# Seven products for gate and value in two blocks, signs masked on VectorE, scores at their own scale

## The chip, the cores and the metric

One core of one Trainium2 chip runs the whole program. The time is the device time of one execution in microseconds (us). The kernel before took 1258.47 us (median of three runs, 1258.27 to 1259.04).

In the profile, PE is TensorE's matmuls, PEld its weight loads, DVE is VectorE, ACT ScalarE, POOL GpSimd and SP SyncE, whose queue issues the DMAs.

## The reference

Attention over 4 batches, 12 heads, 448 tokens and head size 64 (q and k normalised by their root mean square), then two feed-forward stages on the 1792 x 768 result. The inputs are of twice the width of float32 (each number comes as two 32-bit words).

```
q_n, k_n = rmsnorm(q, g_q), rmsnorm(k, g_k)
attn = softmax(q_n @ k_n.T / sqrt(64));  o = attn @ v
x  = o.transpose(0, 2, 1, 3).reshape(1792, 768)
x  = silu(x @ w_in) @ w_out                          # 768 -> 2048 -> 768
y  = (silu(x @ w_gate) * (x @ w_val)) @ w_out2       # 768 -> 1536 -> 768
```

## The kernel before

Nearly every product is done as three float16 matmuls: each operand is split into a high and a low half (hi x hi, hi x lo, lo x hi), summed in PSUM in float32. A weight tile of 128 rows is loaded (one `LDWEIGHTS`) ahead of each matmul.

**The order of the work** is written out by a planner: the class `Plan` gathers operations with the engines they may run on, a planned cost and a due time, and `emit` puts them on the five queues one by one. The table `TUNE` shifts due times (`OFF`, `FINE`) and names the engines that each operation may run on (letters A, D, P for ACT, DVE, POOL, and E for a way by matmuls). Each engine then works through its own queue strictly in that order. A change of `TUNE` therefore reorders everything.

**Stages in time.** Attention of batch 0 with float32 scores (0 to 120 us; four of its six head pairs, `N0 = 4`, feed the float32 matmuls of L701). From 120 us the first feed-forward product of batch 0 (`ffn1_h`, L1011) runs while the weights `w_out` are brought in; its second product (`ffn1_o`, L1051) starts near 229 us, and needs the scales of all 16 pieces of `w_out`. Then attention of batches 1 to 3 runs between the feed-forward products of the batch before. The second feed-forward stage starts near 708 us: four blocks of tokens, of 512, 512, 512 and 256. In each block `ffn2_gv` makes gate and value (L1206), and `ffn2_out` multiplies by `w_out2` (L1250 to L1252). The steady part runs from about 792 us to the end at 1258 us.

**Gate and value of one block** (`ffn2_gv`): for each of 12 column groups f of 128, six weight tiles of gate and six of value, each with three matmuls, 36 matmuls of 512 columns (256 in the last block). Then ACT makes silu (L1211), DVE multiplies with value from PSUM (L1213), ACT rounds to float16 (L1216), DVE makes the remainder (L1217), POOL or ACT scales it (L1218, L1219). `bring_x2` fetches the block's 768 x n inputs from DRAM (`x2d`) and splits them (L832, L842) during the output product of the block before.

**Weights** (`bring`): a 128 x 768 piece arrives by DMA with 64 bits a number. The exponent part is scaled by ACT, DVE or POOL (L873 to L875). The sign and the lowest bits follow one of two ways, named per piece by a letter in `TUNE`: with A or P, DVE shifts the low word (L885) and ACT (L887) or POOL (L888) rescales the high word; with D, DVE masks the sign (L879) and shifts a half word (L880). L890 joins the parts on DVE, and L892 sums the squares on ACT. `convert` then scales and splits the piece (L832 to L842), or makes its low half by matmuls with a diagonal (`pe_lo`, L676), for which `diag` writes the diagonal on POOL (L905).

**Softmax** (`softmax_pair`): DVE takes the negative row maximum of the scores (L715), a small operation scales it (L718 ACT, L719 DVE or L720 POOL), and the exponential reads scores, scale and bias (L723).

Of the kernel before, what the change touches and what calls it, by code (L numbers as in the profile page):

```python
# [45 lines left out]
    GK=('D', 'P', 'DP'),
# [1341 lines left out]
```

## Time and profile before

| what | value |
|---|---|
| median of three runs | 1258.47 us |
| the profiled execution | 1259.7 us, of which 1257.9 us are the span from the first to the last instruction |
| mean granted TensorE clock | 0.98 of full |
| PE busy, share of the span | 94% |
| DVE, ACT, POOL busy | 55%, 53%, 39% |
| DMA issues from SP's queue | the heaviest pieces are 768 KB weights |

Busy times are averages over stages with different limits, so they are to be read by stretch. A matmul's record lasts longer than the step from one matmul to the next, since matmuls are pipelined; the pace is read from runs of matmuls without a gap in the chain of work that ended last.

### The profile page before, as it was taken

Reading aid. Unit: us, or ns where it says so; the run is one execution under the profiler, and the core shown is the slowest. Engines: PE = TensorE matmul, PEld = TensorE weight load, DVE = VectorE, ACT = ScalarE, POOL = GpSimd, SP = SyncE. Lnnn points to the kernel's source line nnn. Section 1 sums busy time; section 2 is a strip of 40 time slices with the busy share of each in tenths; the row PEclk is TensorE's granted clock in tenths of the full one; section 3 lists DMA queues with packets and bytes.
Section 4 is the critical chain, followed back from the end, with each engine's and each line's share of the span. In section 5 each row is a group of like instructions: output and inputs, shape, how many; then the busy total and the mean of one; then the engine's idle time right before and its main releaser. Section 6 shows DMA issues by size and latency. Waiting matters only on the chain.

```text
span 1257.9 us, 17505 instructions
## 1 busy us (share of the span) xinstructions
PE 1178.2 (94%) x6612; PEld 599.2 (48%) x6612; DVE 687.2 (55%) x1181; ACT 669.4 (53%) x1219; POOL 492.0 (39%) x474
## 2 busy tenths in 40 slices
PE   5989987799679999999999999999999999999998
PEld 3334443344334444444445454445544555446685
DVE  4788876688756575565459887873111301112121
ACT  4989967677669865898536435652111301112131
POOL 5565456454658897677721624120000100000000
PEclk9999999799889999999999999999999999999999
DMA  7565634479877688567774455502000101000101
GB/s 193 167 155 144 220 131 145 103 174 199 184 149 144 125 191 176 110 126 149 145 238 138 146 173 180 187 1 63 26 14 1 34 26 26 1 1 22 39 1 26
DMA packets 218581, 140.61 MB, mean 112 GB/s; under 512 B 156032, under 2 KB 210816, under 8 KB 218496
## 3 DMA queue, kind: packets, MB, share of 16 engines
q1 hardware_dynamic: 218496, 139.49, 44.3%
q8 instruction: 52, 0.85, 0.3%
q14 instruction: 33, 0.27, 0.1%
HBM read 85.79 MB, written 11.01 MB: 77 GB/s over the span
## 4 chain that ended last, share of the span: by engine, by line
PE 46%; DVE 5%; DMA 2%; POOL 1%; ACT 1%; issue 1%; POOLq 0%; ACTq 0%
PE ps L1206 25%; PE ps L1051 6%; PE ps L1250 4%; PE ps L1252 4%; PE ps L1251 4%; DMA ATT<-in_moe_w_val_dram 1%; DVE W L842 1%; PE ps L816 1%; PE ps L1011 1%; PE ps L706 1%; DVE ATT L890 1%; DVE G L1030 1%; DVE ATT L880 1%; DVE ATT L879 1%; DMA ATT<-ATT 1%
## 5 line engine op out<-in xcount | busy, mean ns | idle before, releaser
L1206 PE MATMUL ps<-XT,W 128*128 128x512 f16 (+1 forms) x1440 | 294.0, 352 | 3.8 <-ACT ER L1211 1.9
L1051 PE MATMUL ps<-G,W 128*128 128x448 f16 x1152 | 240.7, 355 | 4.0 <-DVE G L1041 4.0
L1011 PE MATMUL ps<-XT,W 128*128 128x448 f16 x1152 | 234.9, 353 | 8.2 <-ACT FT L1017 1.7
L1206 PEld LDWEIGHTS <-W 128*128 128x128 f16 x1440 | 141.0, 98 | 131.0 <-issue 5.1
L1011 PEld LDWEIGHTS <-W 128*128 128x128 f16 x1152 | 110.7, 99 | 120.5 <-issue 26.0
L1051 PEld LDWEIGHTS <-W 128*128 128x128 f16 x1152 | 107.9, 98 | 122.3 <-issue 28.9
L1216 ACT ACTIVATE G<-ER 128x512 f16<-128x512 f32 (+1 forms) x48 | 27.6, 575 | 167.3 <-DVE ER L1213 162.2
L1213 DVE SCALAR_TENSOR_TENSOR ER<-ER,ST,ps 128x512 f32<-128x512 f32 (+1 forms) x48 | 32.6, 680 | 151.5 <-PE ps L1206 151.4
L723 ACT ACTIVATE ER<-ps,ST 128x448 f32<-128x448 f32 x144 | 103.1, 719 | 12.1 <-POOL ATT L745 8.8
L1218 POOL TENSOR_SCALAR G<-ER 128x512 f16<-128x512 f32 x20 | 12.6, 629 | 245.5 <-DVE ER L1217 241.2
L715 DVE TENSOR_REDUCE ST<-ps 128x2 f32<-128x896 f32 x96 | 92.4, 966 | 27.8 <-PE ps L706 23.4
L1250 PE MATMUL ps<-W,G 128*128 128x384 f16 x308 | 100.4, 326 | 0.0
L1251 PE MATMUL ps<-W,G 128*128 128x384 f16 x308 | 100.4, 326 | 0.0
L1252 PE MATMUL ps<-W,G 128*128 128x384 f16 x308 | 100.4, 326 | 0.0
L1257 DVE SCALAR_TENSOR_TENSOR ATT<-ps,ST,ATT 128x384 f32<-128x384 f32 x28 | 17.3, 618 | 151.0 <-ACT ATT L1255 151.0
L1255 ACT ACTIVATE ATT<-ps,ST 128x384 f32<-128x384 f32 x28 | 16.2, 580 | 136.7 <-PE ps L1252 136.7
L745 POOL TENSOR_TENSOR ATT<-ER,ATT 128x448 f16<-128x448 f32 x77 | 86.0, 1117 | 6.4
L706 PE MATMUL ps<-ATT 128*64 128x448 f16 x560 | 75.3, 371 | 9.1 <-ACT ER L723 4.0
L1030 DVE SCALAR_TENSOR_TENSOR G<-FT,ST,G 128x448 f16<-128x448 f32 x64 | 57.5, 907 | 20.1 <-ACT G L1022 18.2
L744 POOL TENSOR_SCALAR ER<-ER,ST 128x448 f32<-128x448 f32 x77 | 56.7, 736 | 22.8 <-ACT ATT L739 11.8
L1206 PE MATMUL ps<-XT,ATT 128*128 128x512 f16 (+1 forms) x288 | 60.4, 352 | 0.0
L739 ACT ACTIVATE ATT<-ER,ST 128x448 f16<-128x448 f32 x71 | 45.5, 660 | 20.0 <-DVE ST L731 11.7
(221 smaller groups left out, 1889.4 us busy)
## 6 DMA issues: line engine op xcount, KB each, us to landing
ATT<-in_moe_w_out_dram SPq DMA_DIRECT2D x24, 768.0 KB, 4.3
W<-in_moe_w_in_dram SPq DMA_DIRECT2D x16, 768.0 KB, 6.1
ATT<-in_moe_w_gate_dram SPq DMA_DIRECT2D x12, 768.0 KB, 4.7
ATT<-in_moe_w_val_dram SPq DMA_DIRECT2D x12, 768.0 KB, 5.9
ATT<-in_q_dram SPq DMA_DIRECT2D x24, 224.0 KB, 3.1
ATT<-in_k_dram SPq DMA_DIRECT2D x24, 224.0 KB, 3.6
ATT<-in_v_dram SPq DMA_DIRECT2D x8, 672.0 KB, 7.2
x2d<-FT SPq DMA_DIRECT2D x24, 224.0 KB, 3.5
```

What stands on the lines that cost most here:

```text
L706: nc.tensor.matmul(out=sp[64 * h:64 * h + 64, u, 0:S], lhsT=T[:, 0, t, 64 * h:64 * h + 64], rhs=T[:, a, :, 64 * h:64 * h + 64], start=(a = ...
L715: op(DVE, 1.04 * S * nt + 65, lambda sp=sp, nm=nm, nt=nt: nc.vector.tensor_reduce(nm, sp[:, 0:nt, 0:S], AX.X, ALU.max, negate=True), r=sk, ...
L723: op(ACT, 705, lambda e=e, u=u, t=t, sp=sp: nc.scalar.activation(e, sp[:, u, 0:S], AF.Exp, bias=st["nb"][:, t:t + 1], scale=eS, accum_out= ...
L744: nc.gpsimd.tensor_scalar(e, e, r1, 1.0, ALU.mult, ALU.mult)
L745: nc.gpsimd.tensor_tensor(lo, e, hi, ALU.subtract)
L1011: nc.tensor.matmul(out=ps[:, 0:S], lhsT=w[:, a, kk], rhs=xt1((b * HP + kk) % NX, x), start=(kk == 0 and s == 0), stop=(kk == KD - 1 and s ...
L1030: DVE: (t_stt(S), lambda gt=gt, hi=hi, lo=lo, s1=s1: nc.vector.scalar_tensor_tensor(lo, gt, s1, hi, ALU.mult, ALU.subtract), True),
L1051: nc.tensor.matmul(out=ps[:, 0:S], lhsT=w[:, a, P * m:P * m + P], rhs=GV1[:, f, x], start=(f == 0 and s == 0), stop=(f == NF1 - 1 and s == 2))
L1206: nc.tensor.matmul(out=ps[:, 0:n], lhsT=w[:, aa, kk], rhs=xt2(kk, x)[:, 0:n], start=(kk == 0 and s == 0), stop=(kk == KD - 1 and s == 2))
L1250: nc.tensor.matmul(out=ps[:, 0, 0:384], lhsT=hi, rhs=wh, start=(f == 0), stop=(f == NF2 - 1))
L1251: nc.tensor.matmul(out=ps[:, 1, 0:384], lhsT=hi, rhs=wlo, start=(f == 0), stop=False)
L1252: nc.tensor.matmul(out=ps[:, 1, 0:384], lhsT=lo, rhs=wh, start=False, stop=(f == NF2 - 1))
```

## The change

**Seven products.** The blocks keep their sizes, but blocks 1 and 2 (counted from 0) compute gate and value by a scheme with seven half-size products in place of eight. The input of a block is a 2 x 2 arrangement (two halves of 256 tokens, two halves of the 768 inputs); so is the weight of one f (two halves of the inputs, gate and value). Seven products of sums of such quarters give the four quarters of the result. Each product has three weight tiles and three matmuls for each, of 256 columns: 63 matmuls an f.

- `make_sums` (new) makes, for each f, four sums of weight quarters in float32 on DVE (ten additions of 384 columns, L1288 of the changed kernel), rounds them on ACT, makes the remainder on DVE (1536 columns, L1297) and stores hi and lo to a DRAM buffer `s2d` (768 KB an f).
- `bring_sums` (new) takes the place of `bring_x2` for the two blocks: three steps, each with two DMAs of 256 KB, four sums of input quarters (256 columns, L1264) and a split of 1792 columns.
- `ffn2_seven` (new) takes the place of `ffn2_gv` there: it loads the sums of each f back from `s2d` into one of two buffers, issues the products (L1329), and joins them in five DVE additions that read PSUM (L1346: three of 256 columns, two of 512). All eight PSUM banks take part.
- The output tiles `OT` shrink from four buffers to two, and `DG` and `FT` become parts of one tile `FD`, whose space the joins use later.

**Signs.** The table `WOS` names D for all 16 pieces of `w_out` (before: one piece by D alone). `diag` may run on DVE as well.

**Scores.** For the first four head pairs the scale stays in the scores: the maximum is the bias itself, and the small scaling operation is left out.

**The tables.** `TUNE` is new in nearly all entries, so that work shifts between ACT, DVE and POOL elsewhere too.

```diff
-    WOS=('P', 'P', 'P', 'AP', 'P', 'A', 'AP', 'AP', 'P', 'P', 'P', 'AP', 'AP', 'AP', 'P', 'D'),
+    WOS=('D',) * 16,
...
-    small(mult(gc, gc, g_s), ["gs"], ["gc"], 0)
+    small(lambda: nc.vector.tensor_scalar(gc, gc, 2.0 ** -25, None, ALU.mult), [], ["gc"], 0)
...
-            op(DVE, 1.04 * S * nt + 65, lambda sp=sp, nm=nm, nt=nt: nc.vector.tensor_reduce(nm, sp[:, 0:nt, 0:S], AX.X, ALU.max, negate=True),
-               r=sk, w=[("nm", i, g)], due=due)
+            own = n < N0
+            top = nb if own else nm
+            op(DVE, 1.04 * S * nt + 65, lambda sp=sp, top=top, nt=nt: nc.vector.tensor_reduce(top, sp[:, 0:nt, 0:S], AX.X, ALU.max, negate=True),
+               r=sk, w=[("nb" if own else "nm", i, g)], due=due)
+            if not own:
...
-        op(POOL, 351, lambda: nc.gpsimd.tensor_scalar(dg, ID, s1, 2.0 ** 14, ALU.mult, ALU.mult), r=["id"] + sk, w=[("dgw", c)], due=due)
+        add({POOL: (351, lambda: nc.gpsimd.tensor_scalar(dg, ID, s1, 2.0 ** 14, ALU.mult, ALU.mult)),
+             DVE: (200, lambda: nc.vector.tensor_scalar(dg, ID, s1, 2.0 ** 14, ALU.mult, ALU.mult), True)}, r=["id"] + sk, w=[("dgw", c)], due=due)
...
+    def make_sums():
...
+            for dst, terms in ((0, ((vh[:, lo], vh[:, hi], ALU.add), (vl[:, lo], ALU.add), (vl[:, hi], ALU.add))),
+                               (2, ((gh[:, lo], vh[:, lo], ALU.subtract), (gl[:, lo], ALU.add), (vl[:, lo], ALU.subtract))),
+                               (1, ((us[:, 0], gh[:, lo], ALU.subtract), (gl[:, lo], ALU.subtract))),
+                               (3, ((gh[:, hi], us[:, 1], ALU.subtract), (gl[:, hi], ALU.add)))):
...
+            op(SP, t_dma(P * 6144), lambda f=f: nc.sync.dma_start(out=s2d[P * f:P * f + P], in_=SH), r=["SHh", "SHl"], w=[("s2d", f)], due=due, late=DMA_LATE)
...
+    RING = [(PS_F[i], ("F", i)) for i in range(3)] + [(PS_X, "psx")] + [(PS_S[i][:, u], ("S", i, u)) for i in range(2) for u in range(2)]
...
+    def ffn2_seven(i, z):
...
+            op(SP, t_dma(P * 6144), lambda sb=sb, f=f: nc.sync.dma_start(out=sb, in_=s2d[P * f:P * f + P]), r=[("s2d", f)], w=sbk, due=t0 + step * (f - 2), late=DMA_LATE)
...
+                for kk in range(KH):
+                    def mm(kk=kk):
+                        for s, (aa, xx) in enumerate(((0, 0), (0, 1), (1, 0))):
+                            c = 1792 * xx + h * x
+                            nc.tensor.matmul(out=ps[:, h * o:h * o + h], lhsT=w[:, aa, kk], rhs=XW[kk][:, c:c + h],
...
+            b1, b6, b2, b57, b34 = take(), take(), take(), take(), take()
+            product(b1, 0, g[:, :, 0:KH], gk, 0)
...
+            product(b6, 0, sw[:, 1], sbk, 2)
+            plus(3, 1, b6, 0, 0, zk[0:1])
+            product(b2, 0, g[:, :, KH:KD], gk, 5)
+            plus(0, 1, b2, 0, 0, zk[0:1])
+            product(b57, 0, sw[:, 0], sbk, 1)
+            product(b57, 1, sw[:, 2], sbk, 3)
+            plus(1, 2, b57, 0, None, zk[3:4])
+            plus(3, 1, b57, 0, 2, zk[2:3])
+            product(b34, 0, sw[:, 3], sbk, 6)
+            product(b34, 1, v1[:, :, KH:KD], vk, 4)
+            plus(1, 2, b34, 0, 1, [])
...
-        ffn2_gv(i, zone(i))
+        (ffn2_seven if i in SEVEN else ffn2_gv)(i, zone(i))
+        if i == 0:
+            plan.tag = "sums"
+            make_sums()
```

**What moves in the queues.** In the listings below a row is an instruction in the order of its queue: line, operation, tile written <- tiles read, size of the output; lines are those of the kernel named, and those of the changed kernel are higher (its L882, L887, L888, L898, L914 do what L874, L879, L880, L890 and, on POOL, L905 do before).

DVE while pieces of `w_out` are converted, of before (L1030 is the low half of `ffn1_h`, L450 to L457 are scales):

```order
L885 TENSOR_SCALAR ATT<-ATT 128x768
L890 SCALAR_TENSOR_TENSOR W<-W,ATT 128x768
L1030 SCALAR_TENSOR_TENSOR G<-FT,ST,G 128x448
L450 TENSOR_SCALAR ST<-ST 128x1 x2
L890 SCALAR_TENSOR_TENSOR W<-W,ATT 128x768
L456 TENSOR_SCALAR ST<-ST 128x1 x2
```

The same place in the changed kernel:

```order
L882 TENSOR_SCALAR W<-ATT 128x768 x2
L887 TENSOR_SCALAR ATT<-ATT 128x768
L914 TENSOR_SCALAR FD<-ID,ST 128x128
L888 TENSOR_SCALAR ATT<-ATT 128x768
L887 TENSOR_SCALAR ATT<-ATT 128x768
L898 SCALAR_TENSOR_TENSOR W<-W,ATT 128x768
```

Sign, half word and join of a piece stand on DVE alone now, and the diagonals stand between them. Counted up to the first matmul of `ffn1_o`, L879 and L880 go from 2 to 17 each, L885 from 30 to 15, L887 on ACT from 16 to 10, L888 on POOL from 14 to 5, and the diagonals on POOL from 15 to 3, with 12 on DVE.

DVE from the output product of block 0 into gate and value of block 1, of before:

```order
L1217 TENSOR_TENSOR ER<-ER,G 128x512
L1257 SCALAR_TENSOR_TENSOR ATT<-ps,ST,ATT 128x384 x6
L1213 SCALAR_TENSOR_TENSOR ER<-ER,ST,ps 128x512
L1217 TENSOR_TENSOR ER<-ER,G 128x512
L1257 SCALAR_TENSOR_TENSOR ATT<-ps,ST,ATT 128x384 x2
```

In the changed kernel, early in block 1 (L1288 and L1297 are the sums of weights of a later f, L1346 the joins, L1364 and L1368 what L1213 and L1217 were):

```order
L1346 TENSOR_TENSOR G<-ps,G 128x512
L1288 TENSOR_TENSOR ATT<-ATT 128x384 x2
L1346 TENSOR_TENSOR FD<-ps,FD 128x256
L1364 SCALAR_TENSOR_TENSOR G<-G,ST 128x512
L1346 TENSOR_TENSOR FD<-ps,FD 128x256
L1346 TENSOR_TENSOR FD<-ps,FD 128x512
L1368 TENSOR_TENSOR G<-G 128x512
L1346 TENSOR_TENSOR FD<-ps,FD 128x256
L1288 TENSOR_TENSOR ATT<-ATT 128x384
L1346 TENSOR_TENSOR FD<-ps,FD 128x512
```

Two instructions an f become seven, and the sums of weights stand between them. By the count in the queues, three of the twelve f have their sums made before the output product of block 0 begins, and the other nine stand in DVE's queue during that product and block 1.

SP's queue at the same place of the changed kernel (L1299 stores sums, L1315 loads them back, L1258 loads inputs, L1412 writes the result):

```order
L1412 DMA out_dram<-ATT 64x768 x2
L1299 DMA s2d<-ATT 128x3072
L1315 DMA ATT<-s2d 128x3072
L1412 DMA out_dram<-ATT 64x768 x2
L1315 DMA ATT<-s2d 128x3072
L1299 DMA s2d<-ATT 128x3072
L1315 DMA ATT<-s2d 128x3072 x2
L1299 DMA s2d<-ATT 128x3072
L1315 DMA ATT<-s2d 128x3072 x3
```

The twelve stores and 24 loads are new, and a load can stand behind a store that waits for a sum.

## Rows read from the trace of the kernel before

**Rows 1.** The page: busy us, share of the span and instructions of each engine.
```profile
PE 1178.2 (94%) x6612; PEld 599.2 (48%) x6612; DVE 687.2 (55%) x1181; ACT 669.4 (53%) x1219; POOL 492.0 (39%) x474
```

**Rows 2.** Busy time by stretch: start:end, length, busy us and instructions, PEclk, DMA.
```profile
120.00:229.00 109.00, 91.53 (x420) 45.22 (x419) 81.38 (x163) 86.98 (x141) 56.19 (x46) 0.94 0.45 149
...
640.00:800.00 160.00, 152.94 (x794) 77.93 (x793) 137.79 (x231) 82.14 (x138) 59.56 (x42) 1.00 0.54 175
800.00:852.00 52.00, 52.00 (x245) 23.72 (x243) 39.46 (x61) 29.95 (x47) 10.00 (x10) 1.00 0.18 61
852.00:992.00 140.00, 140.00 (x721) 70.47 (x720) 27.11 (x38) 25.66 (x40) 8.05 (x13) 1.00 0.08 23
992.00:1132.00 140.00, 140.00 (x721) 70.44 (x720) 27.74 (x40) 26.02 (x41) 7.53 (x12) 1.00 0.07 19
```

**Rows 3.** The chain that ended last: start us, length us, what.
```profile
912.34 80.29 PE ps L1206 x372
...
1187.30 40.61 PE ps L1206 x372
```

**Rows 4.** Groups by form at L1206: count, busy us and mean ns, idle before.
```profile
L1206 PE MATMUL ps<-XT,W 128*128 128x512 f16 x1080 | 249.8, 379 | 3.8 <-ACT ER L1211 1.9 <-ACT FT L1055 1.8
...
L1206 PEld LDWEIGHTS <-W 128*128 128x128 f16 x1440 | 141.0, 98 | 131.0 <-issue 5.1
...
L1206 PE MATMUL ps<-XT,W 128*128 128x256 f16 x360 | 44.2, 273 | 0.0
```

**Rows 5.** Waits of PE from 792 us to the end.
```profile
PE ps L1206 <- ACT ER L1211: 1.9, 1, 1.9
```

**Rows 6.** Groups by form on DVE in gate, value and output.
```profile
L1217 DVE TENSOR_TENSOR ER<-ER,G 128x512 f32<-128x512 f32 x36 | 27.7, 770 | 17.9 <-ACT G L1216 17.8
...
L1213 DVE SCALAR_TENSOR_TENSOR ER<-ER,ST,ps 128x512 f32<-128x512 f32 x36 | 26.9, 746 | 122.3 <-PE ps L1206 122.1
...
L1257 DVE SCALAR_TENSOR_TENSOR ATT<-ps,ST,ATT 128x384 f32<-128x384 f32 x28 | 17.3, 618 | 151.0 <-ACT ATT L1255 151.0
...
L1213 DVE SCALAR_TENSOR_TENSOR ER<-ER,ST,ps 128x256 f32<-128x256 f32 x12 | 5.8, 480 | 29.2 <-PE ps L1206 29.2
...
L1217 DVE TENSOR_TENSOR ER<-ER,G 128x256 f32<-128x256 f32 x12 | 5.1, 425 | 5.8 <-ACT G L1216 5.8
```

**Rows 7.** DVE in order of time: start us, length us, instruction.
```profile
229.64 1.00 DVE L842 SCALAR_TENSOR_TENSOR W<-ATT,ST,W 128x768 f16<-128x768 f32 x1
230.57 1.08 DVE L715 TENSOR_REDUCE ST<-ps 128x2 f32<-128x896 f32 x1
```

**Rows 8.** The page: DMA issues, KB each, median us to landing.
```profile
ATT<-in_moe_w_out_dram SPq DMA_DIRECT2D x24, 768.0 KB, 4.3
...
ATT<-in_moe_w_val_dram SPq DMA_DIRECT2D x12, 768.0 KB, 5.9
```

**Rows 9.** Groups by form at the sign steps and the small scales.
```profile
L880 DVE TENSOR_SCALAR ATT<-ATT 128x768 uint16<-128x768 uint16 x28 | 31.9, 1153 | 0.4
...
L888 POOL TENSOR_SCALAR ATT<-ATT 128x768 f16<-128x768 f32 x14 | 29.2, 2084 | 42.8 <-ACT G L1219 25.5 <-DVE ATT L885 11.3 <-DVE ST L450 3.5
...
L879 DVE TENSOR_SCALAR ATT<-ATT 128x768 int32<-128x768 int32 x28 | 18.9, 681 | 6.7 <-POOL ATT L875 6.1 <-ACT W L873 0.6
...
L885 DVE TENSOR_SCALAR ATT<-ATT 128x768 int32<-128x768 int32 x20 | 13.3, 669 | 0.0
...
L905 POOL TENSOR_SCALAR DG<-ID,ST 128x128 f32<-128x128 f32 x15 | 12.1, 810 | 11.2 <-DVE ST L457 5.8 <-PE ps L677 5.1
...
L719 DVE TENSOR_SCALAR ST<-ST 128x2 f32<-128x2 f32 x10 | 6.0, 613 | 0.0
```

**Rows 10.** Waits of PE, 120 to 233 us.
```profile
PE ps L676 <- POOL DG L905: 12.6, 4, 8.1
PE ps L1051 <- DVE G L1041: 4.0, 1, 4.0
```

**Rows 11.** Waits of DVE, 120 to 229 us.
```profile
DVE W L890 <- POOL W L888: 5.1, 4, 1.8
```

More of the change, by code (lines that the diff above doesn't have):

```diff
@@ L46 @@
[L46 removed]
+    RQ=('P', 'P', 'P'),
+    GK=('P', 'P', 'DP'),
     QL=('D', 'D', 'P'),
[L48 to L49 removed]
+    VH=('DP', 'P', 'A'),
+    VL=('DP', 'P', 'DP'),
     XL=('D', 'D', 'D'),
@@ L886, in bring @@
             add(only(sign, {
-                ACT: (t_act(n) + 60, lambda: nc.scalar.activation(top, wide, AF.Copy, scale=2.0 ** -60)),
-                POOL: (880, lambda: nc.gpsimd.tensor_scalar(top, wide, 2.0 ** -60, 1.0, ALU.mult, ALU.mult))}), r=ykeys, w=skeys, due=need)
+                ACT: (1940, lambda: nc.scalar.activation(top, wide, AF.Copy, scale=2.0 ** -60)),
+                POOL: (2030, lambda: nc.gpsimd.tensor_scalar(top, wide, 2.0 ** -60, 1.0, ALU.mult, ALU.mult))}), r=ykeys, w=skeys, due=need)
             rest = lw
@@ L1065 @@
     NB2 = 512
-    blocks = [(c, min(NB2, NT - c)) for c in range(0, NT, NB2)]
+    blocks = [(0, 512), (512, 512), (1024, 512), (1536, 256)]
+    SEVEN = (1, 2)
+    assert sum(n for _, n in blocks) == NT
+    KH = KD // 2
     O_X, O_ST, O_Y, O_XF = 0, 12288, 30720, 43008
@@ L1072, with t_out2 @@
     T_GV, T_OUT = 94.0, 47.0
+    T_GW = 82.0
     order = [o1slot(c) for c in range(NF1)]
+    def t_out2(i):
+        return t_blk2(i) + (T_GW if i in SEVEN else T_GV) * blocks[i][1] / 512.0
     def t_blk2(i):
-        return T2 + i * (T_GV + T_OUT)
+        return t_out2(i - 1) + T_OUT * blocks[i - 1][1] / 512.0 if i else T2
     def slot2(i):
@@ L1152, in load_w_out2 @@
                 r=[tk], w=key[1:2], due=due + c)
-        marker([("ys", i) for i in range(4)] + [k for c in range(NF2) for k in slot2(2 * NF2 + c)[1]], ["w2_done"])
+        marker([("ys", i) for i in range(2)] + [k for c in range(NF2) for k in slot2(2 * NF2 + c)[1]], ["w2_done"])
     GV2 = G[:, 0:NF2 * 2 * NB2].rearrange("p (f a c) -> p f a c", f=NF2, a=2)
@@ L1220, in ffn2_gv, with other_x, bring_sums @@
                 r=[sk], w=[("Gl", f)], due=-1e4)
+    XU = att32(O_XF, 1792)
+    XW = [XT[:, 3584 * i:3584 * i + 3584] for i in range(2)] + [ER.rearrange("p a c -> p (a c)").bitcast(F16)]
+    def other_x():
+        marker([], [("xf", r) for r in range(4)] + [("xu", 0, a) for a in range(2)] + [("ft2", r) for r in range(3)] + [(k, kk) for k in ("x2h", "x2l") for kk in range(KD)])
+    def bring_sums(i, z, due):
+        c0, n = blocks[i]
+        h = n // 2
+        bs = range(c0 // S, (c0 + n - 1) // S + 1)
+        s = s_x2[z][0]
+        for kk in range(KH):
+            x = 0
+            xu, keys = XU[:, 0:7 * h], [("xf", r) for r in range(4)]
+            for a in range(2):
+                row = P * (kk + KH * a)
+                op(SP, t_dma(P * n * 4), lambda xu=xu, a=a, row=row: nc.sync.dma_start(out=xu[:, 5 * h * a:5 * h * a + n], in_=x2d[row:row + P, c0:c0 + n]),
+                   r=[("x2d", b, kk + KH * a) for b in bs] + ["attn_done"], w=[("xu", x, a)], due=due - 12 + kk, late=DMA_LATE)
+            t = xu.rearrange("p (s c) -> p s c", s=7)
+            ab = [("xu", x, 0), ("xu", x, 1)]
+            for d, a, b, alu in ((3, 6, 1, ALU.subtract), (1, 1, 0, ALU.subtract), (2, 3, 0, ALU.add), (4, 5, 2, ALU.subtract)):
+                add(only(TUNE["XU"], {
+                    DVE: (t_tt(h), lambda t=t, d=d, a=a, b=b, alu=alu: nc.vector.tensor_tensor(t[:, d], t[:, a], t[:, b], alu), True),
+                    POOL: (t_ptt(h), lambda t=t, d=d, a=a, b=b, alu=alu: nc.gpsimd.tensor_tensor(t[:, d], t[:, a], t[:, b], alu))}), r=ab, w=keys, due=due + kk)
+            split(XW[kk][:, 0:7 * h], XW[kk][:, 1792:1792 + 7 * h], xu, keys + ab, s, [("sx2", z), ("silu", B - 1)], [("x2h", kk)], [("x2l", kk)], due + kk, 7 * h)
```

175 lines of the change are left out of this document (126 added, 49 removed).

## The prediction

> **What bounds the kernel now.** I read the page first. PE is busy for 94% of the span and every other engine for about half of it [rows 1]; that share is an average, so next I read busy time by stretch. From 852 us to 1132 us PE has no idle time at all, while DVE works 27 of every 140 us; each of these two stretches holds one output product and one gate-and-value block of 512 tokens. From 640 to 800 us PE is still busy for 152.9 of 160 us, but DVE is at 137.8. In the stretch of 120 to 229 us, where the last weights of the first feed-forward stage are made ready, PE has only 91.5 of 109 us, DVE 81.4 and ACT 87.0 [rows 2]. So the tail is bound by PE alone, the middle by PE with DVE close behind, and the first part by chains that run over all engines. The waits confirm it: from 792 us to the end PE waits once, 1.9 us [rows 5]; in the front it waits 12.6 us for the diagonal that POOL writes, 8.1 us of it at once, and 4.0 us at the start of `ffn1_o` [rows 10].
>
> The chain of waits gives PE's pace without the modelled ends of matmuls: 372 matmuls of 512 columns take 80.29 us, 0.2158 us each, and 372 of 256 columns take 40.61 us, 0.1092 us each [rows 3]. Half the columns cost half the time, and the 256-column form runs with one weight load per matmul, 0.098 us each [rows 4], inside its 0.109 us.
>
> **Seven products, on PE.** One f of a 512 block is 36 matmuls of 512 columns now, 63 of 256 after. A block of 12 f goes from 432 x 0.2158 = 93.2 us to 756 x 0.1092 = 82.5 us. That is 10.7 us a block and 21.4 us for two, all on the engine that has no idle time there [rows 2, 3]. Nothing else on PE changes in the tail; the output products stay.
>
> [...]
>
> **What DVE gets for it.** The joins of an f are three additions of 256 columns from PSUM (0.480 us each, the nearest row), two of 512 (0.746), a product and a remainder of 512 (0.770 each) [rows 6]: 4.47 us in an f of 6.88 us, where before it was 1.5 in 7.8. The sums of weights are ten additions of 384 columns, for which I take the middle of the 256 and 512 rows, 0.598 us, and a remainder of 1536, 2.15 us by the same rows' slope (0.345 us for 256 columns): 8.13 us an f. Three f are done before block 0's output product, by the order of the queues; nine are left for that product and block 1. These two last 140 - 93.2 + 82.5 = 129.3 us on PE [rows 2]. DVE has to do in them: 9 x 8.13 = 73.2, 12 x 4.47 = 53.6, eight output additions at 0.618 = 4.9, twelve sums of inputs at 0.425 = 5.1, and three remainders of 1792 columns at 2.50 (again by slope) = 7.5: 144.3 us, 15.0 more than PE needs. But these are lone durations; instructions that follow at once overlap (one of 1.00 us is followed after 0.93) [rows 7], and with 0.07 us off each of the 206 instructions it is 129.9 us, no more than PE needs. So the bounds are 0 and +15 us. The stretch of 640 to 800 us is the nearest row for an almost full DVE: it costs PE 7.1 us of 160, 4.4% [rows 2]; 4.4% of 129.3 is 5.7. I take +5 us. Block 0's own gate and value take in three f of sums, 24 us, in its second half, about the 52 us from 800 us on, where DVE was idle for 12.5 [rows 2]. DVE's conversions of `w_out2` stay at eighteen instructions by the queues, so the other 12 us are hidden only as far as instructions overlap; the bounds are 0 and +12, and by the same 4.4% of 52 us I take +2. Block 2 has no sums and 53.6 of 82.5 us of DVE, so there I take 0.
>
> [...]
>
> **The way by DRAM.** Each f's sums (768 KB) are stored, and loaded once in each block. Weights of the same size land 4.3 to 5.9 us after issue [rows 8]. A buffer is free after product six of f-1 and wanted at product two of f+1, 9/7 of 6.88 = 8.8 us, so a load has some 3 us to spare. A load that stands behind a store in SP's queue waits for its sum, so a late DVE is passed on to PE through SP too. I count it within the bounds above. The input sums replace splits that already lie under the output product; their three steps must end within its 46.8 us, and PE's queue has the first product in the midst of it. Cost 0, or some us if late, within the same bound.
>
> **Signs and diagonals, 120 to 229 us.** Fifteen pieces of `w_out` leave the way with L885 (0.669 us on DVE) and L887 or L888 (2.08 us on POOL) and take L879 and L880 (0.681 + 1.153 us) [rows 9]. DVE gains 15 x (1.834 - 0.669) = 17.5 us, and 12 diagonals, which it doesn't have before; bounded by nothing and by POOL's 0.810 I take 0.3 each, 3.6 us. POOL loses 9 x 2.08 + 12 x 0.81 = 28 us, ACT six rescales. DVE goes from 81.4 to 102.5 of 109 us. What speaks for a gain: the hand-over between engines goes (L890 waits 5.1 us in four cases for POOL) [rows 11], and with it, perhaps, the 12.6 us for the diagonal. What speaks against: at 94% DVE, with today's share of 75% as the other bound, the stretch would be 102.5 / 0.747 = 137 us, 28 longer. Between -12.6 and +28 I take 0, since the work fits by the shares that DVE holds at 640 us (86%: 119 us, +10) less most of the diagonal's wait.
>
> **Scores.** Sixteen groups of the first four pairs lose a step of about 0.6 us (L719) [rows 9] between maximum and exponential. It lies on a path only where PE waits for the exponential; at most 16 x 0.6 = 10 us, at least 0; I take -2. **The rest of the tables** moves DVE and POOL work by a few instructions in the middle, where PE has little idle time: 0. Two output buffers in place of four: a buffer is wanted again after two tiles, 2 x 11.7 us of PE, and its writes are a quarter the size of those in rows 8: 0.
>
> **Sum.** Profiled execution 1259.7 - 21.4 + 5 + 2 - 2 = 1243.3 us. That execution was 1.2 us above the median of 1258.47, so the forecast for the median is 1242 us.
>
> **Rivals.**
> A. DVE sets the pace from block 0's second half to the end of block 1: the full +15 there and half of the 12, so +21 instead of +7 and 1256 us. For it: the sums leave DVE no slack in the lone durations, queues are strict, and a late sum holds SP's loads too. Against it: overlap, and that DVE's own drains wait for nothing else.
> B. DVE becomes the bound in the front: the stretch of 120 to 229 us grows by 28, so 1270 us, slower than before. It decides from a growth of 16 us on. For it: one engine takes over 21 us of work where it had 28 idle, in strict order with drains that PE waits for. Against it: the pieces' chain no longer changes engines, and POOL, idle more, delays DVE less.
> C. The front gains: the diagonal's 12.6 us go, and DVE keeps up both there and in the tail: 1259.7 - 21.4 - 2 - 12.6 - 1.2 = 1222 us.
> D. Weight loads are not hidden when there are 756 instead of 432 a block: 324 x 0.098 = 31.8 us a block, twice, on top of the forecast, so 1306 us. [...]
> E. The change doesn't do what it says: the joins hold PE just as long in every f of both blocks as the eighth product took, and nothing is seen, 1258 us. Block 2 with DVE at 53.6 of 82.5 us speaks against it.
>
> **How the numbers follow.** Forecast 0.59 (its own range 1231 to 1250), A 0.18, B 0.09, C 0.11, D 0.01, E 0.02. A change of 0.2%, 2.5 us, is about what a measurement can tell from none. Faster: 0.59 + C 0.11 + 0.13 of A = 0.83; within: E and 0.04 of A = 0.06; slower: B, D and the last 0.01 of A = 0.11. The range leaves out B, D, E and the outer ends of A and C: 1224 to 1256 us.
>
> **What would show it.** Right: matmuls of 256 columns at 0.109 us in block 2, its f every 6.9 us; PE idle in blocks 0 and 1 for about 7 us, put down to DVE joins or to loads of sums; the first `ffn1_o` matmul within some 10 us of 229; hardly a wait for the diagonal. Wrong: an f of block 1 well over 7.5 us (A), `ffn1_o` starting past 245 us with DVE over 90% busy ahead of it (B), a pace of 0.2 us in the seven products (D).

## The result, and the profile after

The changed kernel takes 1214.25 us (median of four runs, 1212.89 to 1218.23) against 1258.76 us beside it. The ratio is 0.9652, 95% interval 0.9628 to 0.9676: 3.5% faster. The forecast was 1242 us with a range of 1224 to 1256, so the sign was right, but the time lies below the range: the gain is 44.5 us where 16 were forecast.

The page's busy line of the changed kernel answers to [rows 1]: DVE rose from 55% to 69%, POOL fell from 39% to 34%.

```profile
PE 1146.3 (95%) x7260; PEld 665.0 (55%) x7260; DVE 830.6 (69%) x1492; ACT 711.8 (59%) x1280; POOL 407.3 (34%) x388
```

To find the gain I cut both spans at the same four events: the first weight load of `ffn1_h`, of `ffn1_o`, of gate and value, and of the first output product (that of block 0). The view is busy time by stretch (start:end, length, busy us and instructions of PE, PEld, DVE, ACT and POOL, granted clock, DMA share, GB/s). Before:

```profile
0.00:120.00 120.00, 95.65 (x528) 47.46 (x529) 88.98 (x158) 94.72 (x188) 69.15 (x75) 0.94 0.61 167
120.00:228.80 108.80, 91.44 (x420) 45.12 (x418) 81.18 (x163) 86.98 (x141) 56.07 (x46) 0.94 0.45 149
228.80:708.20 479.40, 450.47 (x2664) 212.38 (x2663) 323.44 (x558) 337.01 (x640) 300.79 (x294) 0.98 0.72 158
708.20:852.20 144.00, 140.25 (x689) 67.61 (x688) 116.21 (x185) 72.34 (x116) 49.99 (x38) 1.00 0.42 138
852.20:1257.90 405.70, 400.42 (x2318) 226.63 (x2316) 77.42 (x121) 78.38 (x137) 15.96 (x24) 1.00 0.08 21
```

After:

```profile
0.00:111.80 111.80, 91.04 (x521) 47.25 (x522) 87.39 (x150) 90.68 (x185) 55.62 (x62) 0.95 0.66 178
111.80:217.80 106.00, 90.17 (x427) 45.16 (x425) 94.13 (x203) 82.82 (x145) 22.17 (x20) 0.94 0.49 158
217.80:682.80 465.00, 445.24 (x2664) 215.26 (x2663) 325.24 (x577) 342.61 (x646) 294.00 (x280) 0.99 0.75 164
682.80:823.00 140.20, 139.96 (x690) 67.55 (x689) 121.73 (x207) 80.37 (x120) 32.83 (x25) 1.00 0.44 149
823.00:1211.00 388.00, 379.88 (x2966) 289.75 (x2964) 202.17 (x358) 115.36 (x186) 2.69 (x4) 1.00 0.28 90
```

The span lost 46.9 us: 8.2 in the front, 2.8 while `w_out` is made ready, 14.4 in the middle, 21.5 in the last two stretches, the tail. Note the middle: 2664 matmuls before and after, yet 14.4 us less.

In the tail the seven products run at the pace of [rows 3]. The chain of waits (start us, length us, what) has 0.1092 us a matmul in block 1 (first row) and block 2, with 0.098 us weight loads as in [rows 4]:

```profile
899.95 55.57 PE ps L1329 x509
...
1007.24 77.62 PE ps L1329 x711
```

And PE waits for next to nothing. These are all its waits from 680 us to the end (us in total, times, longest), to be read against [rows 5]; most of the 8.1 us that PE is idle in the last stretch lies behind its last matmul:

```profile
PE ps L1401 <- ACT G L1235: 1.1, 1, 1.1
PE ps L1401 <- DVE ATT L1408: 1.0, 2, 0.8
PE ps L1403 <- ACT G L1238: 0.4, 1, 0.4
```

No wait on a sum's load, none on a join. From 112 to 218 us the diagonal's wait shrank from the 12.6 us of [rows 10], but a wait for ACT took much of its place:

```profile
PE ps L457 <- ACT ATT L522: 7.3, 1, 7.3
PE ps L681 <- POOL FD L913: 4.7, 1, 4.7
```

DVE's groups by form, 770 to 980 us, show what its tail work costs (mean ns of one is the second number after the bar; then the idle time before). [Rows 6] had 770 ns for an addition of 512 columns and 480 for a join of 256.

```profile
L1288 DVE TENSOR_TENSOR ATT<-ATT,W 128x384 f32<-128x384 f32 x70 | 37.6, 565 | 0.2
L1297 DVE TENSOR_TENSOR ATT<-ATT 128x1536 f16<-128x1536 f32 x12 | 21.1, 1755 | 4.7 <-ACT ATT L1293 4.7
...
L850 DVE SCALAR_TENSOR_TENSOR XT<-ATT,ST,XT 128x1792 f16<-128x1792 f32 x4 | 8.3, 2081 | 1.9 <-ACT XT L840 1.9
L1346 DVE TENSOR_TENSOR FD<-ps,FD 128x512 f32<-128x512 f32 x12 | 8.3, 690 | 2.5 <-PE ps L1329 2.1
...
L1346 DVE TENSOR_TENSOR FD<-ps,FD 128x256 f32<-128x256 f32 x18 | 7.6, 422 | 1.3 <-ACT G L1362 1.1 <-PE ps L1329 0.2
```

### The profile page after: what moved, and what is told of

Read it like the earlier page. It is cut to its first block, busy times and chain, and to the rows that moved or that the text cites. A ratio compares the mean times of both kernels' runs of the same rounds, so it can differ in the third digit from the quotient of the medians.

```text
span 1211.0 us, 19225 instructions
## 1 busy us (share of the span) xinstructions
PE 1146.3 (95%) x7260; PEld 665.0 (55%) x7260; DVE 830.6 (69%) x1492; ACT 711.8 (59%) x1280; POOL 407.3 (34%) x388
## 4 chain that ended last, share of the span: by engine, by line
PE 58%; DVE 2%; ACT 1%; DMA 0%; issue 0%; DVEq 0%; ACTq 0%
PE ps L1329 14%; PE ps L1060 10%; PE ps L1225 10%; PE ps L1020 9%; PE ps L1401 4%; PE ps L1403 4%; PE ps L1402 4%; PE ps L711 1%; PE ps L824 1%; DVE ATT L1288 1%; DMA ATT<-in_moe_w_out_dram 0%; DVE ATT L1165 0%; DVE ATT L1297 0%; DVE ER L1236 0%; ACT ER L731 0%
## 5 line engine op out<-in xcount | busy, mean ns | idle before, releaser
L1060 PEld LDWEIGHTS <-W 128*128 128x128 f16 x1152 | 108.5, 98 | 119.6 <-issue 24.5
L1020 PEld LDWEIGHTS <-W 128*128 128x128 f16 x1152 | 110.5, 98 | 113.6 <-issue 18.4
L1225 PE MATMUL ps<-XT,W 128*128 128x512 f16 (+1 forms) x720 | 130.2, 326 | 0.2
L1329 PEld LDWEIGHTS <-ATT 128*128 128x128 f16 x972 | 95.1, 98 | 12.7
L1225 PEld LDWEIGHTS <-W 128*128 128x128 f16 x720 | 70.4, 98 | 47.5 <-issue 1.1
L1329 PE MATMUL ps<-XT,ATT 128*128 128x256 f16 x648 | 95.5, 273 | 0.0
L753 POOL TENSOR_TENSOR ATT<-ER,ATT 128x448 f16<-128x448 f32 x75 | 82.4, 1098 | 6.3
L1039 DVE SCALAR_TENSOR_TENSOR G<-FD,ST,G 128x448 f16<-128x448 f32 x64 | 54.5, 867 | 11.6 <-ACT G L1031 11.2
L1329 PEld LDWEIGHTS <-W 128*128 128x128 f16 x540 | 52.8, 98 | 7.6
L1329 PE MATMUL ps<-XT,W 128*128 128x256 f16 x360 | 56.2, 273 | 0.0
L747 ACT ACTIVATE ATT<-ER,ST 128x448 f16<-128x448 f32 x73 | 46.5, 660 | 15.8 <-DVE ST L739 10.1
```

The source lines that it names most:

```text
L753: nc.gpsimd.tensor_tensor(lo, e, hi, ALU.subtract)
L1020: nc.tensor.matmul(out=ps[:, 0:S], lhsT=w[:, a, kk], rhs=xt1((b * HP + kk) % NX, x), start=(kk == 0 and s == 0), stop=(kk == KD - 1 and s ...
L1060: nc.tensor.matmul(out=ps[:, 0:S], lhsT=w[:, a, P * m:P * m + P], rhs=GV1[:, f, x], start=(f == 0 and s == 0), stop=(f == NF1 - 1 and s == 2))
L1225: nc.tensor.matmul(out=ps[:, 0:n], lhsT=w[:, aa, kk], rhs=xt2(kk, x)[:, 0:n], start=(kk == 0 and s == 0), stop=(kk == KD - 1 and s == 2))
L1329: nc.tensor.matmul(out=ps[:, h * o:h * o + h], lhsT=w[:, aa, kk], rhs=XW[kk][:, c:c + h], start=(kk == 0 and s == 0), stop=(kk == KH - 1 a ...
```

## The experiments

Unless it says otherwise, an edit keeps the order of all queues, so that only the named work changes. The table gives the five stretches of each run (us, cut at the same events in the profiled execution) and the median of its timed runs. Nine runs with the changed kernel's order have a middle between 465.0 and 469.2 us; a difference of 4 us there is not read.

| kernel | front | `w_out` | middle | block 0 | rest | median |
|---|---|---|---|---|---|---|
| before | 120.0 | 108.8 | 479.4 | 144.0 | 405.7 | 1258.5 |
| after | 111.8 | 106.0 | 465.0 | 140.2 | 388.0 | 1214.3 |
| e1 no seven | 111.7 | 105.7 | 469.2 | 140.9 | 407.9 | 1236.6 |
| e2 old tables | 112.2 | 119.5 | 472.0 | 142.2 | 409.5 | 1257.9 |
| e3 new tables, old code | 120.8 | 121.2 | 498.9 | 148.1 | 405.1 | 1297.8 |
| e4 signs back | 112.8 | 116.7 | 465.6 | 139.9 | 389.2 | 1226.2 |
| e5 scores back | 115.7 | 104.9 | 465.9 | 140.0 | 388.1 | 1216.3 |
| e6 all back | 116.1 | 118.9 | 465.6 | 140.7 | 408.0 | 1251.3 |
| e7 diagonal on POOL | 112.0 | 105.3 | 467.1 | 139.8 | 387.9 | 1213.9 |
| e8 before + signs | 120.0 | 105.9 | 479.3 | 144.1 | 405.7 | 1256.9 |
| e9 remainder twice | 112.5 | 105.4 | 467.1 | 140.2 | 402.9 | 1230.0 |
| e10 before + scores | 112.8 | 109.0 | 480.0 | 144.2 | 405.7 | 1253.5 |
| e11 old due times | 109.6 | 121.0 | 485.7 | 139.9 | 418.1 | 1276.1 |
| e12 old letters | 111.6 | 114.9 | 474.8 | 141.0 | 395.8 | 1241.3 |
| e13 POOL beside | 112.6 | 105.8 | 465.5 | 140.1 | 389.5 | 1215.9 |
| e14 input sums on POOL | 111.3 | 105.3 | 465.7 | 140.4 | 393.1 | 1218.4 |

**Seven products alone** (order kept up to block 0).

```diff
-    SEVEN = (1, 2)
+    SEVEN = ()
-            make_sums()
```

> The changed kernel with gate and value of all four blocks made by the eight-product way and no sums; tables, signs and scores stay new. Theory 1 (the seven products bring 21 us in the tail, and the other 23 us come from ahead of the tail): 1214 + 21 = 1235 us, first gate-and-value matmul still near 683 us, and the part from there to the end 549 us as in the kernel before. Rival (the sums or joins cost something that was hidden in the total, so that the rest of the change is worth more): the tail gets longer by clearly less than 21 us, 1225 us or below.

The ratio to before is 0.9813 (0.9798 to 0.9828). The tail grows from 528.2 to 548.8 us: the seven products are worth 20.6 us, against 21.4 us of PE time in the forecast. Theory 1 holds; all the stalls and the sums together cost under 1 us. Two output buffers in place of four cost nothing either: e1 keeps two, and its tail is 548.8 us against 549.7 before.

**Tables and code crossed.** Two kernels, both with an order of their own.

```diff
# e2: the changed kernel
-TUNE = dict(... new ...)
+TUNE = dict(... old ..., SU='D', SUH='A', XU='DP')
# e3: the kernel before
-TUNE = dict(... old ...)
+TUNE = dict(... new ..., WOS=old)
```

> The changed kernel's code with the tables of the kernel before, so also with the old way of the signs of w_out; seven products and the scores at their own scale stay. Theory 1 (what came ahead of the tail, 8 us before 120 us, 3 up to the first ffn1_o matmul, 13 in the middle, is due to the new tables and the order they give): 1258 - 21 = 1237 us, first gate-and-value matmul near 705 us. Rival 2 (the new code itself, that is scores without the scaling step, brings the 8 us of the front): about 1229 us, first ffn1_h matmul near 112 us.

> The kernel before with the tables of the changed one, but the old ways of the signs of w_out; no seven products, scaling step of the scores kept, diagonal on POOL. Theory 1 (tables): 1258 - 24 = 1235 us, first gate-and-value matmul near 684 us. Rival 2 (scores): 1258 - 16 = 1242 us, with the front up to the first ffn1_h matmul at 120 us. Rival 3 (signs and diagonals, which leave POOL and ACT free): no gain up to 230 us and some in the middle, 1245 us.

No theory holds: the ratios are 0.9988 (0.9972 to 1.0004) and 1.0298 (1.0271 to 1.0324). The new tables make the old code 39 us slower, and the new code with old tables loses nearly all its gain, though its front, 112.2 us, is as short as rival 2 said. These tables fit one program and bring nothing to the other. In e2 my rival A is seen at last: the first sum starts at 815.1 us, 111 us after the first gate-and-value matmul (92 in the changed kernel, whose `OFF` has a new entry of -29 for `sums`), and PE waits for sums (PE's waits, 700 us to the end):

```profile
PE ps L1329 <- DMA ATT<-s2d: 4.9, 3, 4.0
PE ps L1402 <- POOL W L1170: 2.8, 1, 2.8
PE ps L1401 <- DVE G L1346: 2.3, 1, 2.3
```

**Signs.** e4 puts the rescale of 15 pieces back on POOL and ACT in the changed kernel; e7 puts only the diagonals back on POOL; e8 masks the signs in the kernel before.

```diff
# e4
-    WOS=('D',) * 16,
+    WOS=('DP', 'DP', 'DP', 'DA', 'DP', 'DA', ...),   # DVE shift, then a rescale on POOL (P) or ACT (A)
# e7
-             DVE: (200, lambda: nc.vector.tensor_scalar(dg, ID, s1, ...
+             DVE: (200, lambda: nc.gpsimd.tensor_scalar(dg, ID, s1, ...
# e8, in the place of the rescale
+                nc.vector.tensor_scalar(hw, hw, -0x80000000, None, ALU.bitwise_and)
+                nc.vector.tensor_scalar(half_words[:, :, 2], half_words[:, :, 1], 13, None, ALU.logical_shift_right)
```

> The changed kernel with the signs of 15 pieces of w_out made the old way again (9 rescales on POOL, 6 on ACT), in the same places of the queues. Theory 1 (tables): the stretch up to the first ffn1_o matmul changes by no more than 3 us, total 1214 to 1217 us. Rival 3 (signs): the stretch from the first ffn1_h matmul to the first ffn1_o matmul grows by 8 us or more, total 1222 us or more. My own old upper bound (masking makes DVE the limit) would make this run faster than the changed kernel.

> The changed kernel with the diagonals that DVE writes written by POOL again, in the same places of the queues; the signs stay masked on DVE. Theory 1 (the masked signs bring the 12 us by themselves, since the chain of a piece no longer waits for a rescale of 2 us on another engine): within 3 us of the changed kernel, 1214 to 1217 us. Rival (a good part is the diagonal, which no longer stands behind other work in POOL's queue): the wait of the low-half matmul for the diagonal grows from 5 to over 10 us and the total is 1220 us or more.

> The kernel before, its queues in their old order, with mask and half-word shift on DVE for the 15 pieces of w_out (both in the place of the rescale) and nothing else changed. Theory 1 (the masked signs bring some 11 us whatever the order): first ffn1_o matmul near 218 us instead of 229, total 1247 us. Rival (they bring it only in an order that was made for them; here DVE's steps stand ahead of drains that PE waits for): 228 us or later, total 1257 us or more, which is my old rival of a slower front at a smaller size.

e4 (0.9735, 0.9719 to 0.9752) is 11.9 us slower than the changed kernel, 10.7 of it in this stretch: the signs matter. e7 (0.9620, 0.9603 to 0.9638) is the same as the changed kernel, so the diagonals do not. e8 (0.9962, 0.9945 to 0.9978) gains 2.9 us in the stretch, between its two theories. DVE works more in the stretch and is not in the way (stretch rows as above, e4, then e8):

```profile
112.80:229.50 116.70, 93.14 (x427) 45.64 (x425) 88.97 (x188) 92.10 (x151) 42.80 (x29) 0.93 0.44 144
```

```profile
120.00:225.90 105.90, 90.73 (x420) 45.23 (x419) 89.01 (x178) 78.81 (x136) 35.70 (x36) 0.95 0.47 154
```

**Scores.** e5 puts the small step back in the changed kernel, e10 takes it out of the kernel before.

```diff
# e5
+                if own and g % 2:
+                    nc.vector.tensor_scalar(nb, nm, eS, None, ALU.mult)
+                elif own:
+                    nc.gpsimd.tensor_scalar(nb, nm, eS, 1.0, ALU.mult, ALU.mult)
# e10
-    small(mult(gc, gc, g_s), ["gs"], ["gc"], 0)
+    small(lambda: nc.vector.tensor_scalar(gc, gc, 2.0 ** -25, None, ALU.mult), [], ["gc"], 0)
-                POOL: (246, lambda nm=nm, nb=nb: nc.gpsimd.tensor_scalar(...
+                POOL: (246, (lambda: None) if n < N0 else lambda nm=nm, nb=nb: nc.gpsimd.tensor_scalar(...
```

> The changed kernel with the scaling step between maximum and exponential put back for the first four head pairs (odd groups on DVE, even ones on POOL), in the same places of the queues. Theory 1 (the 8 us ahead of 120 us come from the removed step, since the first batch is a chain in which each group waits for it): 16 steps on the path, first ffn1_h matmul at 117 to 120 us instead of 111.8, total 1220 to 1222 us. Rival (the order given by the tables brought them): first ffn1_h at 112 to 113 us, total 1214 to 1216 us. My own old estimate for the step, 2 us, is nearer to the rival.

> The kernel before, its queues in their old order, with the first four head pairs' scores at their own scale and without the scaling step. Theory 1 (the step brings 4 us in any order, as putting it back cost 4): first ffn1_h matmul at 116 us instead of 120, total 1254 us. Rival (it brings them only in the new order): 119 to 120 us, total 1258 us.

e5 (0.9640, 0.9625 to 0.9655) lengthens the front by 3.9 us, between its two theories, but its total is only 2 us above the changed kernel, which the spread of runs hardly tells from it. e10 (0.9958, 0.9943 to 0.9973) shortens the old front by 7.2 us: its theory 1, with more in the front than the 4 us it named. The step lies on the path, more in the old order than in the new. In e10's front PE has 2.1 us less idle time than before, and is busy 5.1 us less for the same work, at a granted clock of 0.98 instead of 0.94. That the clock rose with the shorter waits is not shown: the changed kernel and e9, with one order there, have 0.95 and 0.98 in fronts of 111.8 and 112.5 us.

```profile
0.00:112.80 112.80, 90.52 (x527) 46.39 (x528) 84.86 (x148) 91.99 (x188) 67.70 (x69) 0.98 0.64 173
```

**What the order alone is worth.** e6 undoes seven products, signs, scores and diagonals together and keeps the order (up to block 0, as e1). The new layout of `FD` and the two output buffers stay in it.

```diff
-    SEVEN = (1, 2)
+    SEVEN = ()
-    WOS=('D',) * 16,
+    WOS=('DP', 'DP', 'DP', 'DA', ...),
+    and the edits of e5 and e7
```

> The changed kernel with the order of its queues, but eight products, the old way of the signs, the scaling step and the diagonal on POOL. What is left of the change is the order that the new tables give. Theory 1 (seven products 21 us, signs 12, scores 8 make the whole gain of 44): 1255 us. Rival (the order alone brings the 14 us between the first ffn1_o matmul and the first gate-and-value matmul): that stretch stays at 465 us and the total is 1242 to 1247 us.

It is at 1251.3 us (0.9919, 0.9899 to 0.9939), and both answers are half right. The middle stays at 465.6 us, 13.8 less than before, as the rival says; but the stretch of `w_out` is 10.1 us longer than before, so that the total lies between the two.

```profile
116.10:235.00 118.90, 96.63 (x427) 46.77 (x426) 80.53 (x177) 92.14 (x151) 49.57 (x40) 0.91 0.44 142
235.00:700.60 465.60, 446.51 (x2664) 215.44 (x2663) 325.98 (x577) 342.49 (x646) 293.85 (x280) 0.98 0.75 164
```

**Which half of the tables.** The changed code with old due times (and other numbers), or with old letters. Here the order is free.

```diff
# e11
-    FINE, OFF, CUT, SLACK, PATIENCE, T_ATT, STEP, ... new
+    the same, old; OFF['sums'] stays -29
# e12
-    WIY, WOY, PHI1, RK, VL, WIH, GVY, O2L, ... new
+    the same, old; WOS stays ('D',) * 16
```

> The changed kernel's code and engine letters with the due times and other numbers of the old tables (the offset of the sums stays at -29). Theory 1 (the due times, which set the order, bring the 14 us between the first ffn1_o matmul and the first gate-and-value matmul): that stretch 475 to 480 us instead of 465, total 1224 us or more. Rival (the letters, which say what engine does what, bring them): that stretch stays near 465 us.

> The changed kernel's code and due times with the engine letters of the old tables (the signs of w_out stay masked). Theory 1 (due times bring the middle's 14 us): the stretch between the first ffn1_o matmul and the first gate-and-value matmul stays near 465 us. Rival (letters): 475 us or more. In the tail, old letters give POOL more of w_out2 and of the input sums: if DVE's additions take longer beside POOL's, block 1 ends later by up to 10 us.

Ratios 1.0129 (1.0105 to 1.0152) and 0.9859 (0.9835 to 0.9884). e11 is for its theory 1, with more in the middle than it named, e12 for its rival, at 474.8 just short of the 475. The middle loses 20.7 us with old due times and 9.8 with old letters. Its matmuls do not change in number by more than 8; PE's idle time does (e11, then e12; length less PE busy is 34.0 and 24.9 us, against 28.9 before and 19.8 after). e11 loses elsewhere too, 15.0 us while `w_out` is made ready and 30.1 in the last stretch, where PE waits 12.7 us for the remainders of input sums, made on POOL (L848):

```profile
230.60:716.30 485.70, 451.66 (x2672) 217.38 (x2672) 303.31 (x523) 339.31 (x635) 334.45 (x333) 0.97 0.72 155
```

```profile
226.50:701.30 474.80, 449.92 (x2668) 213.84 (x2667) 329.42 (x589) 340.54 (x644) 273.89 (x256) 0.97 0.72 160
```

**DVE's slack in the tail.**

```diff
-                DVE: (t_tt(1536), lambda: nc.vector.tensor_tensor(sl, US, sh, ALU.subtract), True),
+                DVE: (t_tt(1536), lambda: [nc.vector.tensor_tensor(sl, US, sh, ALU.subtract) for _ in range(2)], True),
```

> The changed kernel with the remainder of the weight sums (1536 columns, 1.76 us each on DVE) made twice: 21 us more work for DVE, 15.8 of it between the first output product and the end of block 1. Theory 1 (the stall did not come because additions and remainders are shorter than I took them, 0.56 instead of 0.60 and 1.76 instead of 2.15 us, and DVE keeps some 12 to 18 us idle there): no more than 4 us longer, 1214 to 1218 us. Rival (DVE was just at PE's pace, as in my old sum, where 130 us of work stood against 129 of PE): all of it comes out, 1228 to 1231 us.

1230.0 us (0.9760, 0.9732 to 0.9788). My theory 1 fell: 14.9 us come out. That is close to the 15.8 us of the nine repeats that run from the first output product on, which the rival expected to come out in full, but it is made up in another way. Compared matmul by matmul with the changed kernel, from the first output product on, PE is 9.0 us late after 21 us of the changed kernel's time, when five repeats have run (8.8 us of work, three of the five in block 0), and 13.9 us late after 63 us, when eight have (14.0 us). The last four, 7.0 us of work, cost 1.0. So DVE had nothing to spare from the sums in block 0 up to the second f of block 1, and at least 6 us behind that. The rows of e9 show where PE is idle: 11.6 us before 900 us, at a granted clock of 0.98, and 0.3 in the next 72.

```profile
825.20:900.00 74.80, 63.17 (x401) 39.34 (x400) 70.50 (x107) 23.05 (x26) 1.60 (x2) 0.98 0.37 128
900.00:972.00 72.00, 71.72 (x657) 63.80 (x655) 67.43 (x116) 29.78 (x45) 0.62 (x1) 1.00 0.45 161
```

The extra work delays what stands behind it in DVE's queue, and output products wait for that first (PE's waits, 750 us to the end):

```profile
PE ps L1403 <- ACT G L1238: 4.2, 2, 3.8
PE ps L1401 <- ACT G L1235: 2.9, 2, 1.8
PE ps L1401 <- DVE ATT L1408: 2.8, 3, 1.7
PE ps L1329 <- DVE XT L850: 1.7, 2, 1.5
```

**POOL beside DVE.** In the traces of the changed kernel, e2, e11 and e12 a 384-column addition on DVE takes 0.55 us with POOL idle, and in the mean 0.73, 0.90, 0.98 and 0.81 us beside POOL's steps of 256 columns or more (7, 30, 22 and 14 additions; worked out from both engines' instructions in order of time). e13 adds small POOL instructions, e14 moves the input sums to POOL.

```diff
# e13, at each addition of weight sums from the fourth f on
+            for _ in range(2):
+                nc.gpsimd.tensor_scalar(GX, GX, 1.0, 1.0, ALU.mult, ALU.mult)
# e14
-                    DVE: (t_tt(h), lambda ...: nc.vector.tensor_tensor(t[:, d], t[:, a], t[:, b], alu), True),
+                    DVE: (t_tt(h), lambda ...: nc.gpsimd.tensor_tensor(t[:, d], t[:, a], t[:, b], alu), True),
```

> The changed kernel with 180 small instructions on POOL (64 columns, a product by one on a tile that nothing reads any more), two beside each addition of the weight sums from the fourth f on; POOL is otherwise nearly empty there. Their nearest row is a POOL step of 128 columns, 0.68 us, so 0.3 to 0.7 us each. Theory 1 (DVE's additions of operands in SBUF take longer when POOL works at the same time: 0.94 instead of 0.55 us, as seen in the kernel with old tables): the 384-column additions come out at 0.75 us or more in the mean, DVE has about 1 us to spare, and the total is 1224 to 1245 us. Rival (those long additions had another cause, such as transfers): they stay at 0.56 us and the total at 1214 us.

> The changed kernel with all 24 sums of inputs (256 columns, two operands in SBUF) issued on POOL, in the same places of the queues: 0.92 us each there, 0.42 us each on DVE, which has 10 us less to do. Theory 1 (DVE's additions are held up by a POOL instruction that moves 256 columns or more, not by any POOL instruction): 384-column additions beside these sums at 0.75 us or more, against 0.55 us alone, and PE no better off, 1213 to 1218 us. Rival (POOL is no cause): they stay at 0.55 us beside the sums too.

e13 (0.9664, 0.9643 to 0.9685) is for its rival: 87 us of small POOL work hardly lengthen the additions. The 78 beside it take 0.573 us, the 36 with POOL idle 0.551; the largest group goes from 0.565 to 0.577 us (groups by form, 770 to 980 us; DVE, then POOL):

```profile
L1293 DVE TENSOR_TENSOR ATT<-ATT,W 128x384 f32<-128x384 f32 x70 | 38.6, 577 | 0.2
```

```profile
L1274 POOL TENSOR_SCALAR GX<-GX 128x64 f32<-128x64 f32 x180 | 86.7, 482 | 14.8
```

e14 (0.9678, 0.9653 to 0.9703) is for its theory 1: the 12 additions that run beside a 256-column POOL sum take 0.79 us in the mean, the 103 with POOL idle 0.548, and the total is about 4 us up though DVE has 22 additions (9 us) less. Whether the longer additions cost the 4 us, or the sums themselves, 0.90 us each on POOL for 0.42 on DVE, is not separated. POOL in the same view:

```profile
L1264 POOL TENSOR_TENSOR ATT<-ATT 128x256 f32<-128x256 f32 x21 | 18.6, 897 | 85.7 <-DMA ATT<-x2d 77.5 <-DVE ATT L1288 7.4
```

No experiment points to a kernel faster than the changed one; e7 is its equal.

## Why the prediction was wrong, point by point

The forecast for the profiled execution was 1243.3 us, and it took 1212.9. By the table and the forecast's terms, the 30 us are 14.4 in the middle, 7.1 in the tail, 6.2 in the front and 2.8 while `w_out` is made ready.

**Seven products: right.** 21.4 us forecast, 20.6 measured (e1), at the pace of [rows 3, 4].

**The stalls of the tail, +7: mis-sized, they are under 1 us.** The step that failed is the surcharge of 4.4%, taken from the stretch of 640 to 800 us [rows 2]. That stretch holds the end of the attention and the last of the first feed-forward stage, whose waits have other owners. In the tail a DVE busy for 94% costs PE 0.2 us (first row, from 823 us on). The third row is the whole stretch of the sum, block 0's output product and block 1:

```profile
823.00:850.00 27.00, 26.79 (x163) 15.77 (x162) 25.40 (x43) 10.36 (x13) 0.00 (x0) 1.00 0.42 141
850.00:878.00 28.00, 28.00 (x189) 18.27 (x188) 25.32 (x42) 10.40 (x10) 1.60 (x2) 1.00 0.36 123
823.00:956.40 133.40, 133.19 (x1063) 103.83 (x1062) 118.30 (x208) 53.39 (x72) 2.21 (x3) 1.00 0.45 153
```

So the central count, 129.9 us of DVE work for 129.3 of PE, was too high: DVE is busy for 118.3 of 133.4 us. The instructions themselves were shorter than my rows: 0.56 for 0.598 us, 1.755 for 2.15, 2.08 for 2.50, joins 0.42 and 0.69 for 0.48 and 0.746. The 770 ns of [rows 6] was a mean over 29 instructions with POOL idle (0.695) and 7 beside POOL, up to 1.65 us, and I drew the slope through it. Even so DVE had nothing to spare in the first half of this stretch (e9). The count gave one figure for all of it and could not show that; that it came out at PE's pace is luck.

**Scores, -2: mis-sized.** 4 us in the new order (e5), 7 in the old (e10), inside the bound of 10. I priced only the wait; e10's front has a granted clock of 0.98 for 0.94 besides.

**The front, up to 120 us.** I gave it no term but the scores'. The order by itself brings 3.9 us there (e6: 116.1 us), the scores by themselves 7.2 (e10), both together 8.2: they do not add up.

**Signs and diagonals, 0: near in size, -2.8 us, by luck.** The new order without the signs costs 10.1 us in that stretch (e6) and the signs win 11 to 13 back (e4, e6), two effects that I had not seen and that nearly cancel; in the old order the signs by themselves win 2.9 (e8). The diagonals are worth nothing (e7). Rival B fell: DVE held 89% of the stretch without cost.

**"The rest of the tables: 0": the step that failed most, -14.4 us.** I looked at how many instructions move and at PE's small share of idle time. But the middle had 28.9 us of idle time, and it is 19.8 after; and idle time was paid for again where the granted clock fell beside it. Before, it is 0.96 in the first stretch of the middle and 0.91 in the second:

```profile
228.80:310.40 81.60, 75.45 (x460) 35.02 (x459) 65.99 (x125) 55.67 (x116) 41.71 (x38) 0.96 0.83 173
310.40:409.20 98.80, 82.38 (x475) 38.45 (x474) 65.66 (x109) 74.24 (x136) 65.36 (x59) 0.91 0.80 161
```

After, 0.98 and 0.95:

```profile
217.80:291.60 73.80, 71.53 (x438) 34.47 (x437) 61.29 (x108) 47.98 (x99) 44.63 (x42) 0.98 0.79 169
291.60:390.70 99.10, 82.18 (x490) 39.62 (x489) 69.09 (x119) 76.31 (x143) 66.92 (x61) 0.95 0.85 172
```

The granted clock is at a lower level, 0.50 of full, in three pieces of the middle before. They begin inside PE's gaps of 4.0 us (from 228.9) and 3.7 us (from 328.3), and at the end of one of 2.3 us (from 340.9):

```profile
230.50:237.30 6.80, 4.37 (x14) 1.39 (x14) 6.80 (x19) 4.82 (x10) 2.77 (x2) 0.50 0.50 137
329.50:336.30 6.80, 4.27 (x22) 2.25 (x22) 4.22 (x8) 3.01 (x8) 4.76 (x4) 0.50 0.92 179
343.20:353.40 10.20, 7.19 (x34) 2.83 (x34) 5.08 (x9) 4.63 (x12) 6.04 (x4) 0.50 0.93 193
```

These are 23.8 us; after, there are 13.7. The 14.4 us of the middle are 9.2 of idle time and 5.2 of busy time for the same 2664 matmuls (450.5 and 445.2 us). An estimate from the rows puts 3 of the 5.2 to the clock: PE was busy at the lower level for 15.8 us before and 9.8 after, at about half the pace (22 matmuls of L816 take 4.32 us there, from 332.03 us, and 2.27 at the full clock, from 312.91). What the other 2 are stays open. That the order, with the engines it names, does it and not the new code is shown from both sides: in e4, e5 and e6 the middle stays at 466 us whatever is put back, and in e8 and e10, in the old order, at 479 to 480 us with new code. No run separates the order from the new layout of `FD`, though the operations there wait on its parts as they did on `FT` and `DG`. Which of its many moves does it stays open: due times and letters both count, and neither alone (e11, e12).

**The rivals.** C, the front gaining, was nearest in total, and half of it came true: the tail did not stall, but most of what the diagonal's wait lost, a wait for ACT took. A is seen in e2: from the second f of block 1 to the second of block 2 it takes 146.4 us instead of 129.3 (907.2 to 1053.6, 879.9 to 1009.3 us). That the earlier sums of the changed kernel avoid it is likely but not shown, since e2 differs in all its tables. D and E fell with the pace of 0.1092 us, at which every matmul has its weight load of 0.098 us; D's load on top of each matmul was an assumption that no run shows.

## What to carry to other kernels

A retuned table of due times is a change of its own: cut the span at the same events, count the idle time that the order could still remove and what a lower granted clock costs beside it, and take that as the bound rather than zero. Before a mean duration is used as a price, split it by what the other engines did beside it. A busy share does not tell an engine's slack until work is added: e9's repeats showed none in one half of a stretch where DVE was busy for 89%, and 6 us in the other.
